# Order of a Strassen-style second MLP product against the LN2 of the next rows

## The chip, the cores and the metric

The kernel runs on one core of one Trainium2 chip. The metric is device time in microseconds (us) for one execution of the whole kernel; a kernel's time is the median of several executions. The engines run their own instruction streams and meet at semaphores: TensorE (PE in the profile) for matrix products, VectorE (DVE), ScalarE (ACT), GpSimd (POOL), and SyncE (SP), whose queue issues the DMA transfers. Each engine takes its compute instructions in the order in which the program gives them (this kernel is scheduled by hand: the order of the calls in the Python source is the order on every engine).

## The reference

One pre-norm block over 2048 rows of 576 values: a sliding dilated attention with 32 heads, then an MLP with 4608 hidden values, both with a residual. Cut to what matters here:

```python
def _layernorm(x): ...                       # mean and variance over the 576 columns
def _B_ref(x, w1, b1, w2, b2):
    y = _layernorm(x)
    h = _gelu(einsum("bsd,df->bsf", y, w1) + b1)
    return einsum("bsf,fd->bsd", h, w2) + b2

h  = x + _A_ref(_layernorm(x), wqkv, wo)     # _A_ref: attention, then the product with wo
h2 = h + _B_ref(_layernorm(h), w1, b1, w2, b2)
return h2
```

Operands are bf16; the MLP's inner `_layernorm` and the one in front of it are folded into one (called LN2 below).

## The kernel before

The 16 tiles of 128 rows are worked off in eight pairs (`GROUPS`). For each pair the MLP has two steps. `mlp1` makes the hidden values: PE products into PSUM (`pm`), GELU on ACT into `hT`. Then comes the product with w2. For the last two pairs, the seventh and the eighth, this second product is done as a Strassen-Winograd scheme with seven products instead of eight blocks' worth (`mlp2_fast`). Each of the seven has 18 matmuls of 128x128 by 128x288.

PSUM is used as four pairs of banks, tagged A, B, C and D:

```python
    def psum_pair(tag, name, dtype=F32):
        n = 512 if dtype == F32 else 1024
        return psum.tile([P, 2, n], dtype, tag=f"ps{tag}", name=name)
...
        PLAN = {
            "pair": [[([0], "A"), ([1], "B")], [([2], "D"), ([3], "C")], [([4], "A"), ([5], "B")],
                     [([6], "C"), ([7], "D"), ([8], "A")]],        # mlp1: visits and their banks
        }
```

The second product. `a` to `f` are accumulators, one bank each; product 1 is made once in `a` and is copied by ACT to `b`, so that it can be the start of two sums: product 2 is added to `a`, product 6 to `b`.

```python
    def h_sums(v):                  # four DVE sums and differences of hidden values, visit v
        ...
    PRODUCTS = {
        1: (lambda m: h_block(0, 0, m // 2)[:, m % 2, :], lambda m: w2_block(0, 0, m, m + 1)),
        2: (lambda m: h_block(1, 0, m // 2)[:, m % 2, :], lambda m: w2_block(1, 0, m, m + 1)),
        3: (lambda m: s_slot(3, m, m + 1), lambda m: w2_block(1, 1, m, m + 1)),
        4: (lambda m: h_block(1, 1, m // 2)[:, m % 2, :], lambda m: t_slot(3, m, m + 1)),
        5: (lambda m: s_slot(0, m, m + 1), lambda m: t_slot(0, m, m + 1)),
        6: (lambda m: s_slot(1, m, m + 1), lambda m: t_slot(1, m, m + 1)),
        7: (lambda m: s_slot(2, m, m + 1), lambda m: t_slot(2, m, m + 1)),
    }                               # s_slot: what h_sums wrote; t_slot: sums of w2, made earlier

    def product(n, bank, start, m0=0, m1=None): ...         # 18 matmuls into one bank

    def mlp2_fast(g, tags, last, ahead):
        j0, j1 = g
        call(ahead)
        h_sums(len(VISITS) - 1)
        af, b, ce, d = (psum_pair(tag, "po") for tag in tags)
        a, f, c, e = (pair[:, n, 0:HALF] for pair in (af, ce) for n in range(2))
        b, d = b[:, 0, 0:HALF], d[:, 0, 0:HALF]
        bank = {1: a, 2: a, 3: f, 4: c, 5: d, 6: b, 7: e}
        ...
        then = {
            1: [c_(nc.scalar.copy, b, a)],
            6: [c_(nc.scalar.copy, d, b)],
            2: [c_(add, o0[:, lo], a, x_all[:, j0, lo])] + ...,
            5: ..., 3: ...,
        }
        then.setdefault(6 if last else 7, []).extend([c_(residual), c_(add, o1[:, lo], c, rest[:, lo])])
        ...
        if last:
            order = [(1, 0, cut), (4, 0, cut), (1, cut, NM), (4, cut, NM)] + [(n, 0, NM) for n in (7, 6, 2, 5, 3)]
        else:
            order = [(n, 0, NM) for n in (1, 4, 2, 6, 7, 5, 3)]
        for n, m0, m1 in order:
            product(n, bank[n], n in (1, 3, 4, 7), m0, m1)
            if m1 == NM:
                call(then.get(n, ()))
```

For the seventh pair, `ahead` is the work on the rows of the eighth (c and d here are row tiles, not banks): the product with wo into the PSUM pairs B and C, then LN2 for both tiles.

```python
                ia[0] = ia.get(0, []) + [c_(wo_visit, (c, "B"), (d, "C")), c_(ln2_pair, c, d, e)]
...
        def ln2_pair(c, d, e, b2=True):
            for j in (c, d):
                ln2(j)              # DVE: h = pw + x, statistics; reads the PSUM of wo_visit
                ln2_rstd(j)         # POOL: power -1/2
                if j == d:
                    ln2_bias(c)     # DVE
                    send_h(c)       # ACT: hn = normalised h; DMA: to DRAM and back transposed (hnT)
                if b2:
                    add_b2(j)       # DVE
            ...
            ln2_bias(d)
            send_h(d)
```

`hnT` is what the `mlp1` of the eighth pair reads. That step follows the seventh pair's `mlp2_fast` on PE. For the eighth pair `ahead` is empty.

Of the kernel before, what the change touches and what calls it, by code (L numbers as in the profile page):

```python
# [17 lines left out]
def kernel(  # L18
# [12 lines left out]
    nc = tc.nc  # L31
# [13 lines left out]
    HALF = D // 2  # L45
# [45 lines left out]
# [3 lines that stand above are left out]
# [389 lines left out]
    NM = FT // 2  # L483
# [40 lines left out]
    def h_sums(v):  # L524
        m = (2 * VISITS[v][0], 2 * VISITS[v][-1] + 2)
        def op(t, a, b, alu):
            nc.vector.tensor_tensor(out=s_slot(t, *m), in0=a, in1=b, op=alu)  # L527
        a11, a12, a21, a22 = (h_tile[v][:, odd::2, i * P:(i + 1) * P] for i in range(2) for odd in range(2))
        op(0, a21, a22, ALU.add)
        op(1, s_slot(0, *m), a11, ALU.subtract)  # L530
        op(2, a11, a21, ALU.subtract)
        op(3, a12, s_slot(1, *m), ALU.subtract)
# [12 lines left out]
    def product(n, bank, start, m0=0, m1=None):  # L545
        lhs, rhs = PRODUCTS[n]
        for m in range(m0, NM if m1 is None else m1):
            l, r = lhs(m), rhs(m)
            l = l.rearrange("p m c -> p (m c)") if len(l.shape) == 3 else l
            r = r.rearrange("p m c -> p (m c)") if len(r.shape) == 3 else r  # L550
            nc.tensor.matmul(bank, lhsT=l, rhs=r, start=(start and m == 0), stop=(m == NM - 1), skip_group_check=True)  # L551

    def c_(fn, *a):
        return lambda: fn(*a)

    def mlp2_fast(g, tags, last, ahead):
        j0, j1 = g
        call(ahead)
        h_sums(len(VISITS) - 1)
        af, b, ce, d = (psum_pair(tag, "po") for tag in tags)  # L560
        a, f, c, e = (pair[:, n, 0:HALF] for pair in (af, ce) for n in range(2))
        b, d = b[:, 0, 0:HALF], d[:, 0, 0:HALF]
        bank = {1: a, 2: a, 3: f, 4: c, 5: d, 6: b, 7: e}
        o0, o1 = (late.tile([P, D], BF16, tag="o_sb", name="o_sb", bufs=2) for _ in range(2))
        rest, part = (sb.tile([P, D], F32, tag="h", name="rest", bufs=2) for _ in range(2))
        lo, hi = slice(0, HALF), slice(HALF, D)

        def add(out, x, y):
            nc.vector.tensor_tensor(out=out, in0=x, in1=y, op=ALU.add)

        def residual():
            add(rest[:].rearrange("p (g c) -> p g c", g=2), e.unsqueeze(1).to_broadcast([P, 2, HALF]),
                x_all[:, j1, :].rearrange("p (g c) -> p g c", g=2))
            add(rest[:, lo], b, rest[:, lo])

        def store(j, o, cols):
            nc.sync.dma_start(out=out3[:, j, cols], in_=o[:, cols])
# [4 lines that stand above are left out]
            2: [c_(add, o0[:, lo], a, x_all[:, j0, lo])] + ([c_(store, j0, o0, lo)] if last else []),  # L582
            5: [c_(add, o1[:, hi], d, rest[:, hi]), c_(store, j1, o1, slice(0, D)),
                c_(add, part[:, hi], d, x_all[:, j0, hi])],
            3: [c_(add, o0[:, hi], f, part[:, hi]), c_(store, j0, o0, hi if last else slice(0, D))],
        }
        then.setdefault(6 if last else 7, []).extend([c_(residual), c_(add, o1[:, lo], c, rest[:, lo])])
        cut = 12
        if last:
            order = [(1, 0, cut), (4, 0, cut), (1, cut, NM), (4, cut, NM)] + [(n, 0, NM) for n in (7, 6, 2, 5, 3)]  # L590
        else:
            order = [(n, 0, NM) for n in (1, 4, 2, 6, 7, 5, 3)]
        for n, m0, m1 in order:
            product(n, bank[n], n in (1, 3, 4, 7), m0, m1)
            if m1 == NM:
                call(then.get(n, ()))
# [9 lines left out]
    def call(fns):  # L606
        for fn in fns:
            fn()

    with tc.manual_schedule(engines={ENG.PE, ENG.Activation, ENG.DVE, ENG.SP, ENG.Pool}):  # L610
# [167 lines left out]
        def mlp1(grp, plan, ahead, between):  # L778
            for v, duos in enumerate(PLAN[plan]):
                call(ahead.get(v, ()))  # L780
                visit([mlp1_duo(grp, us, tag) for us, tag in duos], None, between.get(v, ()))

        def mlp2_tile(grp, i, tag, inserts):
            po_of[grp[i]] = psum_pair(tag, "po")
            mlp2(i, [po_of[grp[i]][:, half, 0:HALF] for half in range(2)], inserts)
# [17 lines left out]
        for k, g in enumerate(GROUPS):  # L803
            c, d = GROUPS[k + 1] if k + 1 < len(GROUPS) else (None, None)
            e, f = GROUPS[k + 2] if k + 2 < len(GROUPS) else (None, None)
            m1, mid, ia, ib = {}, {}, {}, {}
            m1[0] = []
            if 0 < k <= len(GROUPS) - len(fast):
                m1[0].append(c_(finish_out, GROUPS[k - 1][1]))
            if k == 0:  # L810
                m1[0] += [c_(halos, 1), c_(att_qk_a, d), c_(att_qk_b, d), c_(halo, d, 1)]
                mid[0] = [c_(exps, d)]
                m1[1] = [c_(pv_t, c), c_(pv_t, d), c_(load_w2, 4), c_(att_qk, e)]
                ia[0] = [c_(wo_visit, (c, "B"))]
                ia[12] = [c_(exps, e), c_(wo_visit, (d, "A")), c_(ln2_pair, c, d, e, False), c_(pv_sum, e), c_(dma_tr_o, e), c_(halos, 2)]
                ib[0] = [c_(finish_out, g[0])]
                ib[4] = [c_(att_qk, f)]
                ib[32] = [c_(exps, f)]
            elif c is not None:
                m1[0].append(c_(pv_t, d))  # L820
                if k == 1:
                    m1[0] += [c_(add_b2, j) for j in g]
                if e is not None:
                    m1[3] = m1.get(3, []) + [c_(att_qk, e)] + [c_(w2_sums, *m) for m in T_SUMS.get(k, ())]
                    ia[0] = [c_(exps, e)]
                ia[0] = ia.get(0, []) + [c_(wo_visit, (c, "B"), (d, "C")), c_(ln2_pair, c, d, e)]
                ib[0] = [c_(finish_out, g[0])]
                if e is not None:
                    ia[2] = [c_(pv_sum, e), c_(dma_tr_o, e)]
                    ib[2] = [c_(att_qk, f)] + ([c_(halos, 7)] if k == 1 else [])  # L830
                    ib[32] = [c_(exps, f)]
            if g in fast:
                if g == fast[0]:
                    m1[1] = [c_(w2_sums, 16, NM)]
                for v in range(3):
                    m1[v + 1] = m1.get(v + 1, []) + [c_(h_sums, v)]
            mlp1(g, "pair", m1, mid)
            if g in fast:
                mlp2_fast(g, "DBAC" if c is not None else "BDCA", c is None, ia.get(0, ()))
            else:  # L840
                mlp2_tile(g, 0, "D", ia)
                mlp2_tile(g, 1, "C", ib)
# [30 lines left out]
```

## Time and profile before

| | |
|---|---|
| time, median of 3 | 374.71 us (374.47 to 376.33) |
| span of the profiled execution | 374.5 us |
| PE busy | 364.6 us, 97% of the span |
| DVE busy | 315.9 us, 84% |
| ACT busy | 210.0 us, 56% |
| POOL busy | 26.5 us, 7% |
| mean granted clock of TensorE | 0.993 of full speed |

The page of the profile gives busy time, the chain of work that ended last, and groups of instructions. A group is named by its source line, engine and operation, then by what it writes and reads: "L551 PE MATMUL po<-w2a_sb,hT" are the matmuls of `product` that take their moving operand from `w2a_sb`; `po<-kv_ring,...`, `q_all` and `x_all` are those that take it from the sums of w2, which are kept in buffers no longer needed by the attention. "L554 ACT COPY po<-po" is the copy from one accumulator to another, "L168 ACT ACTIVATE hn" the normalisation of LN2, L402 the DVE addition that opens LN2, L527 the sums in `h_sums`, L204 all products of `mlp1` and wo, L569 the additions that make the output. A time in brackets is how long the engine stood idle before the row, with what released it.

### The profile page before, as it was taken

To read this page: it belongs to the slowest core of one execution; us is meant where nothing else is said; L and a number is where in the kernel's file an instruction comes from. 1 tells how busy PE (TensorE), PEld (TensorE's weight loads), DVE (VectorE), ACT (ScalarE), POOL (GpSimd) and SP (SyncE) were. 2 spreads that over 40 slices of the span, in tenths; PEclk is the share of its full clock that TensorE was granted. 3 is DMA by queue.
4 is the path that set the end of the run, shared out by engine and by line. 5 is a ranking of instruction groups with operands and counts; after the bars stand their busy time and mean duration, and the time that the engine had idled before them with its cause. 6 is when DMAs were issued, how large, how long until landed. Compare 5 with 4: busy or idle time off the path is not lost.

```text
span 374.5 us, 11470 instructions
## 1 busy us (share of the span) xinstructions
PE 364.6 (97%) x4944; PEld 301.0 (80%) x4944; DVE 315.9 (84%) x522; ACT 210.0 (56%) x435; POOL 26.5 (7%) x34
## 2 busy tenths in 40 slices
PE   7999999999999999999999999999999999799996
PEld 3789877887789978887888788878887788578874
DVE  6899999999999999999998999999999995632332
ACT  2688756796509851875187508760876087205630
POOL 2231004000100010002000200020002000200000
PEclk9999999999999999999999999999999999899999
DMA  8969798946335326412411241114110411110000
GB/s 246 311 193 292 186 189 256 338 143 102 125 88 161 38 54 185 156 35 54 102 52 35 55 102 52 35 38 118 52 35 19 109 45 21 39 47 20 4 0 32
DMA packets 57265, 38.96 MB, mean 104 GB/s; under 512 B 31344, under 2 KB 55536, under 8 KB 57216
## 3 DMA queue, kind: packets, MB, share of 16 engines
q1 hardware_dynamic: 57056, 38.18, 37.8%
q8 instruction: 38, 0.62, 0.7%
q14 instruction: 11, 0.09, 0.1%
q10 hardware_dynamic: 160, 0.07, 0.1%
HBM read 19.92 MB, written 12.42 MB: 86 GB/s over the span
## 4 chain that ended last, share of the span: by engine, by line
PE 67%; DVE 26%; issue 2%; POOL 2%; ACT 1%; DMA 1%; POOLq 0%; DVEq 0%
PE pm L204 31%; PE po L480 24%; PE po L551 8%; DVE prod L318 4%; DVE ln_stats L144 4%; PE pw L204 4%; DVE prod L357 3%; DVE prod L312 3%; DVE prod L361 3%; POOL ln_rstd L155 2%; DVE ln_mv L145 1%; PE pq L204 1%; DVE mx L328 1%; DVE h L402 1%; ACT hT L465 1%
## 5 line engine op out<-in xcount | busy, mean ns | idle before, releaser
L204 PE MATMUL pm<-hnT,w_sb 64*128 64x256 bf16 x2304 | 143.2, 269 | 0.6 <-ACT hT L465 0.5
L465 ACT ACTIVATE hT<-pm,b_sb 128x256 bf16<-128x256 f32 (+1 forms) x288 | 108.2, 503 | 34.2 <-PE pm L204 32.2
L204 PEld LDWEIGHTS <-w_sb 64*128 64x128 bf16 x2304 | 113.6, 94 | 14.4 <-issue 2.6
L480 PEld LDWEIGHTS <-hT 128*128 128x128 bf16 x864 | 84.0, 98 | 22.6 <-issue 1.7
L480 PE MATMUL po<-w2a_sb,hT 128*128 128x288 bf16 x672 | 84.5, 286 | 0.0
L204 PE MATMUL pq<-wq_sb,xnT 64*128 64x288 bf16 x768 | 54.1, 283 | 0.3 <-ACT kv_ring L289 0.2
L204 PEld LDWEIGHTS <-xnT 64*128 64x128 bf16 x864 | 44.0, 94 | 9.1 <-issue 0.4
L155 POOL TENSOR_TENSOR ln_rstd<-ln_veps,mhalf 128x1 f32<-128x1 f32 (+2 forms) x27 | 25.8, 957 | 296.1 <-DVE ln_veps L149 247.9
L318 DVE TENSOR_TENSOR prod<-prod 128x2304 bf16<-128x2304 bf16 (+1 forms) x64 | 44.2, 691 | 2.1
L340 ACT ACTIVATE logits<-logits 128x256 f32<-128x256 f32 x16 | 6.7, 417 | 67.9 <-DVE logits L329 67.9
L357 DVE TENSOR_TENSOR prod<-kv_ring,a 128x4608 bf16<-128x4608 bf16 x16 | 40.9, 2558 | 0.3
L312 DVE TENSOR_TENSOR prod<-kv_ring,q_all 128x4608 bf16<-128x4608 bf16 x16 | 40.8, 2552 | 0.2
L204 PE MATMUL pm<-hnT,w1h_sb 64*128 64x256 bf16 x288 | 39.5, 269 | 0.0
L361 DVE TENSOR_TENSOR prod<-prod 128x2304 bf16<-128x2304 bf16 (+1 forms) x32 | 33.9, 1058 | 1.1
L480 PE MATMUL po<-w2b_sb,hT 128*128 128x288 bf16 x192 | 25.5, 286 | 0.0
L289 ACT CAST kv_ring<-pq 128x576 bf16<-128x576 f32 x32 | 19.4, 641 | 8.3 <-PE pq L204 8.2
L168 ACT ACTIVATE hn<-h,ln_nmr,ln_rstd 128x576 bf16<-128x576 f32 x16 | 13.9, 867 | 15.6 <-DVE ln_nmr L164 15.6
L204 PE MATMUL pw<-wo_sb,oT 64*128 64x288 bf16 x256 | 19.5, 283 | 0.2
L438 ACT ACT_TABLE_LOAD x14 | 18.0, 1283 | 0.3
L204 PEld LDWEIGHTS <-oT 64*128 64x128 bf16 x288 | 14.1, 94 | 4.0 <-POOLq L214 0.8
L527 DVE TENSOR_TENSOR prod<-hT 128x512 f16<-128x512 f16 (+1 forms) x8 | 3.6, 455 | 16.1 <-ACT hT L465 16.1
L402 DVE TENSOR_TENSOR h<-pw,x_all 128x576 f32<-128x576 f32 x16 | 12.0, 752 | 5.7 <-PE pw L204 5.7
(88 smaller groups left out, 317.1 us busy)
## 6 DMA issues: line engine op xcount, KB each, us to landing
w_sb<-in_B_w_dram SPq DMA_DIRECT2D x6, 768.0 KB, 6.1
kv_ring<-kv_dram SPq DMA_DIRECT2D x28, 144.0 KB, 2.5
w2a_sb<-in_B_w_dram SPq DMA_DIRECT2D x4, 1008.0 KB, 6.3
kv_dram<-kv_ring SPq DMA_DIRECT2D x13, 288.0 KB, 4.1
out_dram<-o_sb SPq DMA_DIRECT2D x15, 144.0 KB, 2.0
td<-q_all SPq DMA_DIRECT2D x14, 144.0 KB, 2.3
td<-hn SPq DMA_DIRECT2D x14, 144.0 KB, 2.0
wq_sb<-in_A_wqkv_dram SPq DMA_DIRECT2D x3, 576.0 KB, 5.8
```

Source lines behind the costliest of these rows:

```text
L155: nc.gpsimd.tensor_tensor(out=rstd[:], in0=veps[:], in1=mhalf[:].to_broadcast([P, n]), op=ALU.pow)
L204: last = nc.tensor.matmul(duo["g"][r ^ swap][i], lhsT=lhsT, rhs=rhs, start=(swap == 0 and i == 0 and kt == 0), stop=(swap == 1 and kt == K ...
L289: pace[0] = nc.scalar.copy(out=dst.rearrange("p (d g h) -> p g d h", g=2, h=H // 2), in_=ps[:, :, 0:HALF].rearrange("p g (h d) -> p g d h" ...
L312: nc.vector.tensor_tensor(out=prod[:], in0=k_ring[j % 2], in1=q_all[:, j, :].unsqueeze(1) .to_broadcast([P, W, D]), op=ALU.mult)
L318: nc.vector.tensor_tensor(out=prod[:, :, o * H:o * H + n], in0=prod[:, :, a * H:a * H + n], in1=prod[:, :, c * H:c * H + n], op=ALU.add)
L357: nc.vector.tensor_tensor(out=prod[:].rearrange("p w (d h) -> p w d h", h=H), in0=v_ring[j % 2].rearrange("p w (d h) -> p w d h", h=H), in ...
L361: nc.vector.tensor_tensor(out=prod[:, 0:n, :], in0=prod[:, 0:n, :], in1=prod[:, n:2 * n, :], op=ALU.add)
L402: nc.vector.tensor_tensor(out=h[:].rearrange("p (g c) -> p g c", g=2), in0=pw[:, :, 0:HALF], in1=x_all[:, j, :].rearrange("p (g c) -> p g ...
L438: nc.scalar.activation(out=warm[:], in_=mhalf[:], func=ACT.Gelu_apprx_tanh)
L465: pace[0] = nc.scalar.activation(out=hT[us[i // GF]][:, GF * r + i % GF, 0:N], in_=ps[:, r, i * N:(i + 1) * N], func=ACT.Gelu_apprx_tanh, ...
L480: nc.tensor.matmul(banks[half], lhsT=hT[f // (2 * GF)][:, f % (2 * GF), i * P:(i + 1) * P], rhs=w2_rows(f)[:, half * HALF:(half + 1) * HAL ...
L551: nc.tensor.matmul(bank, lhsT=l, rhs=r, start=(start and m == 0), stop=(m == NM - 1), skip_group_check=True)
```

## The change

In the second product of the seventh pair, product 1 and its copy are now issued between the two parts of `ahead`: after the product with wo, ahead of LN2. The rest of the seven products follow after LN2 and `h_sums` as before, without product 1. Because `b` is now taken while B and C still hold the result of the wo product that LN2 has to read, the bank tags are dealt out anew: `b` moves from B to A, and the pair of `c` and `e` from A to B; `a`, `f` and `d` stay where they were. The purpose is that the copy stands ahead of LN2's two normalisations in the order of ACT. The eighth pair's order doesn't change, since its `ahead` is empty and it is excepted by `if not last`.

```diff
     def mlp2_fast(g, tags, last, ahead):
         j0, j1 = g
-        call(ahead)
+        call(ahead[:1])
+        af, b = (psum_pair(tag, "po") for tag in tags[:2])
+        if not last:
+            product(1, af[:, 0, 0:HALF], True)
+            nc.scalar.copy(out=b[:, 0, 0:HALF], in_=af[:, 0, 0:HALF])
+        call(ahead[1:])
         h_sums(len(VISITS) - 1)
-        af, b, ce, d = (psum_pair(tag, "po") for tag in tags)
+        ce, d = (psum_pair(tag, "po") for tag in tags[2:])
         a, f, c, e = (pair[:, n, 0:HALF] for pair in (af, ce) for n in range(2))
...
         else:
-            order = [(n, 0, NM) for n in (1, 4, 2, 6, 7, 5, 3)]
+            order = [(n, 0, NM) for n in (4, 2, 6, 7, 5, 3)]
...
             if g in fast:
-                mlp2_fast(g, "DBAC" if c is not None else "BDCA", c is None, ia.get(0, ()))
+                mlp2_fast(g, "DABC" if c is not None else "BDCA", c is None, ia.get(0, ()))
```

## The prediction

> **What bounds the kernel now.** I read the page first: PE is busy 364.6 of 374.5 us, so only its idle or slow stretches can give time back. The busy shares in 40 slices show one dent late in the run.
>
> ```profile
> PE   7999999999999999999999999999999999799996
> ...
> PEclk9999999999999999999999999999999999899999
> ```
>
> Slice 35 (about 318 to 328 us) has a 7 for PE and an 8 for the clock granted to it: one place, with both an idle stretch and a slow one. It lies in the second product of the seventh pair. The list of who waited for whom, for PE from 295 us to the end, names one wait.
>
> ```profile
> PE po L551 <- ACT po L554: 2.3, 1, 2.3
> ```
>
> So a matmul waited once, for 2.3 us, for the ACT copy of product 1. The timeline of that stretch shows which matmul and why the copy was late.
>
> ```profile
> 317.81 1.89 PE L551 MATMUL po<-w2a_sb,hT 128*128 128x288 bf16 x14
> 319.53 0.65 PE L551 MATMUL po<-w2b_sb,hT 128*128 128x288 bf16 x4
> ...
> 320.02 1.14 PE L551 MATMUL po<-kv_ring,hT 128*128 128x288 f16 x8
> ...
> 321.98 0.41 PE L551 MATMUL po<-kv_ring,hT 128*128 128x288 f16 x2
> ...
> 322.19 0.87 ACT L168 ACTIVATE hn<-h,ln_nmr,ln_rstd 128x576 bf16<-128x576 f32 x1 [3.74 <-DVE ln_nmr L164]
> ...
> 323.46 0.87 ACT L168 ACTIVATE hn<-h,ln_nmr,ln_rstd 128x576 bf16<-128x576 f32 x1 [0.40 <-DVE ln_nmr L164]
> ...
> 324.24 0.39 ACT L554 COPY po<-po 128x288 f32<-128x288 f32 x1
> ...
> 324.68 3.10 PE L551 MATMUL po<-w2a_sb,hT 128*128 128x288 bf16 x14 [2.29 <-ACT po L554]
> 327.57 1.14 PE L551 MATMUL po<-w2b_sb,hT 128*128 128x288 bf16 x4
> ```
>
> Product 1 (w2 blocks: 14 + 4 matmuls) runs from 317.81 and ends at 319.53 + 0.65 = 320.18. Product 4 (w2 sums) fills PE until 322.39. Product 2 comes next and adds to the bank that the copy has to read first. The copy's input is ready at 320.18, but ACT stands 3.74 us idle in front of the first normalisation of LN2, which is ahead of the copy in its order and waits for DVE. The copy starts at 324.24, 4.06 us later than its data allow.
>
> The view by stretches tells what happens to the clock after the gap (columns: stretch, length, busy time and count of PE, PEld, DVE, ACT, POOL, then clock, DMA share, GB/s).
>
> ```profile
> 322.40:324.68 2.28, 0.01 (x1) 0.00 (x1) 1.80 (x5) 1.82 (x3) 0.83 (x1) 1.00 0.24 72
> 324.68:328.50 3.82, 3.82 (x18) 2.50 (x18) 0.74 (x2) 0.00 (x0) 0.00 (x0) 0.56 0.34 86
> 328.50:337.46 8.96, 8.96 (x73) 6.96 (x71) 2.95 (x6) 0.38 (x1) 0.00 (x0) 1.00 0.16 38
> ```
>
> The 18 matmuls of product 2 run at a mean clock of 0.56; cut into half microseconds, the same view has 0.50 in every piece from 325.5 to 328.5, and 0.94 in the next. So the wait costs twice: as a gap, and as a slow product after it.
>
> [...]
>
> **The change, part by part.**
>
> *Removed: the gap.* Matmuls of this shape start every 2.20 / 18 = 0.122 us (in the eighth pair product 2 starts at 364.09 and the next product at 366.29). Product 4's last piece starts at 321.98 and has 2 matmuls, so the next could start at 321.98 + 0.24 = 322.22. It started at 324.68: **2.46 us** lost. (The profile's 2.29 counts from the modelled end.)
>
> *Removed: the slow product.* Product 2 takes from 324.68 to the start of product 6 at 328.53, 3.85 us, against 2.20 us at full clock: **1.65 us** lost. If PE no longer idles, its clock has no reason to fall.
>
> Cross-check: from product 1 to the first matmul of the next mlp1 is 337.46 - 317.81 = 19.65 us. Seven undisturbed products are 7 x 2.20 = 15.40 us, and about 0.24 us of issue time stands ahead of mlp1 in the trace. 19.65 - 15.40 - 0.24 = 4.01 us, against 2.46 + 1.65 = 4.11. I take 4.1.
>
> *Moved: product 1.* On PE it already followed the wo product directly, with only DVE, ACT, POOL and DMA work standing between them in program order. Its place on PE, 317.81, doesn't move: 0 us.
>
> *Moved: the copy.* It should start about 0.09 us after product 1 ends, as in the eighth pair (359.10 to 359.19), so at 320.27, and take 0.39 us, ending near 320.66. Product 2 wants its bank at 322.22, so there are some 1.5 us to spare. ACT is idle from 318.45 (the last GELU, 313.96 + 4.49) to 322.19, so the copy delays no normalisation: 0 us.
>
> *Moved: the banks.* `b` now takes A, last read by GELU on ACT until 318.45, before the copy. `c` takes B, last read by the L402 addition at 317.43 + 0.76 = 318.19; product 4 wants it at 320.02. In the eighth pair's mlp1, A and B are the first pairs wanted, and the last readers of `b`, `c` and `e` are the additions after product 7, all done (335.04 in the old trace) before product 3 is through. The swap costs nothing.
>
> *Added:* no instruction; the counts are the same. Sum: 374.71 - 4.1 = 370.6 us, a ratio of 0.989.
>
> **The rivals.**
>
> 1. *Another wait takes the gap's place: h_sums.* Product 6 moves up to 322.22 + 2.20 = 324.42. Its last third needs the second L527 result of the last visit, which ends at 323.93 + 0.56 = 324.49, and is wanted at 324.42 + 12 x 0.122 = 325.9. Product 7 needs the third (324.95) only after 326.6. Even a wait put on the first matmul would cost 0.1 us. Slack against: 1.4 us. If DVE were 2 us later, the time would be near 371.3 to 372.
>
> 2. *Transposed rows for the next mlp1 arrive late.* The last transpose is issued at 328.70, and the transfer view gives 3.0 us to landing: 331.7. The next mlp1 moves from 337.46 to 333.4. Slack 1.7 us, so a transfer up to that much slower is still hidden. If it came 2 us late, the time would be 371. LN2 itself isn't touched, so I see no reason for that.
>
> 3. *The clock doesn't come along.* If its dip had another cause than the gap, only 2.46 us would be won: 372.3. Against: every long stretch around it stands at 1.00, with the same matmuls and the same load, and the dip begins half a microsecond after the gap.
>
> 4. *The gain is given back at the tail.* The eighth pair's products follow its mlp1 on PE without a wait, and the last output addition ends with product 3. The chain after 324.68 is PE alone (12.86, 17.79 and 15.56 us, then one DVE addition of 0.46). Nothing there is tied to an absolute time, so the shift should arrive whole.
>
> 5. *Slower*: the copy would have to hold up LN2, and LN2 the mlp1, by over 4 us beyond their slack. I see nothing for it.
>
> **Range and chances.** The central value is 370.6. Rivals 1 and 2 in mild form would add up to 1 us, rival 3 makes 372.3; the three times before spread from 374.47 to 376.33, so a median can sit half a microsecond off or more. On the low side there is only the reading error of the sum, a few tenths. I take 370.1 to 371.9. Faster by over 2% would need 7.5 us, where all that can be won here is 4.1; slower by over 2% needs a new wait that I don't find. Chances: 0.01 faster, 0.98 within 2%, 0.01 slower.
>
> **What would show each step right or wrong.** The wait "PE po L551 <- ACT po L554" disappears from the list of PE's waits. The first copy stands at about 320.3, ahead of both hn rows, and these stay at about 322.2 and 323.5. Product 2 starts near 322.2 and takes 2.2 us; the clock is 1.00 from 322 to 334. The next mlp1 starts at about 333.4, the last product's end moves up by 4.1, and the span is about 370.4 us. The prediction is wrong if PE shows a new wait, on L527 or before the first matmul of mlp1, or if the clock still falls to half somewhere in 322 to 330.

## The result and the profile after

The changed kernel takes 372.23 us in the median of four executions (372.02 to 372.65), the kernel before 374.75 us (374.47 to 376.33). The ratio is 0.9926, with a 95% interval of 0.9896 to 0.9955. The prediction was 370.6 us with a range of 370.1 to 371.9: the change is an improvement, as foretold, but of 2.5 us instead of 4.1, and the time lies outside the range.

And yet the trace after looks as the prediction drew it. The page's rows for PE and its clock have lost both dents:

```profile
PE   7999999999999999999999999999999999999996
...
PEclk9999999999999999999999999999999999999999
```

In the list of who waited for whom, PE has no row for L551 any more. The timeline of the stretch (start, length, what) has the copy, now line L562, ahead of both normalisations:

```profile
318.32 1.89 PE L551 MATMUL po<-w2a_sb,hT 128*128 128x288 bf16 x14
...
320.04 0.65 PE L551 MATMUL po<-w2b_sb,hT 128*128 128x288 bf16 x4
...
320.79 0.38 ACT L562 COPY po<-po 128x288 f32<-128x288 f32 x1 [1.83 <-PE po L551]
...
322.49 0.41 PE L551 MATMUL po<-kv_ring,hT 128*128 128x288 f16 x2
...
322.70 0.87 ACT L168 ACTIVATE hn<-h,ln_nmr,ln_rstd 128x576 bf16<-128x576 f32 x1 [1.53 <-DVE ln_nmr L164]
322.74 1.88 PE L551 MATMUL po<-w2a_sb,hT 128*128 128x288 bf16 x14
...
323.97 0.87 ACT L168 ACTIVATE hn<-h,ln_nmr,ln_rstd 128x576 bf16<-128x576 f32 x1 [0.40 <-DVE ln_nmr L164]
...
324.94 1.14 PE L551 MATMUL po<-kv_ring,prod 128*128 128x288 f16 x8
```

This execution is 0.51 us later than the old one when product 1 starts (318.32 against 317.81), for reasons upstream. From there, the copy starts 0.10 us after product 1 ends (320.04 + 0.65 = 320.69), product 2 follows product 4 in the very next slot, and takes 324.94 - 322.74 = 2.20 us. The stretches show the full clock where it was 0.56:

```profile
322.40:324.68 2.28, 2.28 (x21) 1.83 (x19) 1.77 (x7) 1.57 (x2) 0.99 (x1) 1.00 0.10 32
324.68:328.50 3.82, 3.82 (x34) 3.04 (x32) 1.63 (x4) 0.54 (x2) 0.00 (x0) 1.00 0.30 73
```

The chain of work that ended last goes from the wo product through all seven products into the next mlp1 on PE alone (columns: start, length, what):

```profile
316.18 2.21 PE pw L204 x36
318.38 15.54 PE po L551 x126
333.93 17.79 PE pm L204 x324
351.72 15.56 PE po L551 x126
367.30 0.46 DVE o_sb L574
```

Before, it left PE for LN2 and came back through the copy, behind which stood 90 of the 126 matmuls of `product`:

```profile
323.46 0.02 ACT hn L168
...
324.24 0.40 ACT po L554
...
324.68 12.86 PE po L551 x90
```

From product 1 to the next mlp1 there are now 333.93 - 318.32 = 15.61 us, where there were 19.65: 4.04 us less between these two traces, as predicted. The puzzle is therefore not in the kernel after. The two traces differ by 4.0 us in this stretch and by 3.6 us in their spans (374.5 and 370.9), but the two medians only by 2.5 us.

The lead is a pair of numbers for single executions. The profiled execution of the kernel before has a span of 374.5 us and a time of 376.27 us; the other one has 370.9 and 372.65. A time is some 1.8 us longer than the span of the same execution. So the profiled execution of the kernel before was not a 374.7 us one but one of 376.3, although its span looks like the median.

### The profile page after: what moved, and what is told of

Its sections match the earlier page's. It is cut to its first block, busy times and chain, and to the rows that moved or that the text cites. A ratio compares the mean times of both kernels' runs of the same rounds, so it can differ in the third digit from the quotient of the medians.

```text
span 370.9 us, 11469 instructions
## 1 busy us (share of the span) xinstructions
PE 363.7 (98%) x4944; PEld 300.7 (81%) x4944; DVE 316.0 (85%) x522; ACT 209.7 (57%) x435; POOL 26.5 (7%) x34
## 4 chain that ended last, share of the span: by engine, by line
PE 71%; DVE 22%; issue 2%; ACT 1%; DMA 1%; POOL 1%; POOLq 0%; DVEq 0%
PE pm L204 31%; PE po L480 24%; PE po L551 8%; PE pw L204 4%; DVE prod L357 3%; DVE prod L318 3%; DVE prod L312 3%; DVE prod L361 3%; DVE ln_stats L144 2%; PE pq L204 2%; DMA kv_ring<-kv_dram 1%; PE busy L636 1%; POOL ln_rstd L155 1%; DVE mx L328 1%; ACT hT L465 1%
## 5 line engine op out<-in xcount | busy, mean ns | idle before, releaser
L527 DVE TENSOR_TENSOR prod<-hT 128x512 f16<-128x512 f16 (+1 forms) x8 | 3.6, 455 | 16.0 <-ACT hT L465 16.0
```

## The theory and its rivals

**Theory T**: the gap on PE is there in every execution of the kernel before, and costs 2.46 us. The half clock after it, 1.65 us, is met only in some; the profiled one was among them, and the median of four was not. **R1**: all 4.1 us are won in every execution, and the new banks or the moved product lose 1.6 us again. **R2**: every gap, however short, brings the clock down. **R3**: the clock's fall has nothing to do with the length of the gap. **R4**: it comes from the wait or the load after it, not from PE's idleness.

In all, 101 more executions of the kernel before were timed beside the experiments. They fall into two groups with nothing between: 56 with a mean granted clock of 0.998 to 1.000 and a median of 374.70 us (374.41 to 375.70), and 45 with 0.993 to 0.995 and a median of 376.41 us (376.09 to 378.01). The medians lie 1.71 us apart; product 2 at half clock had been worked out as 1.65. The profiled execution of the kernel before has (1 - 0.56) / 0.5 x 3.82 = 3.4 us at half clock; that takes about 3.4 x 0.5 / 374.5 = 0.005 off the mean clock, which is the distance between the groups. Below, "with the clock down" means an execution of the second kind; where in the run its clock was down is seen in the profiled executions alone. The time exceeds the span by 1.79 us in the mean of the 101 (1.73 to 1.86).

## The experiments

### The copy put back

```diff
             product(1, af[:, 0, 0:HALF], True)
-            nc.scalar.copy(out=b[:, 0, 0:HALF], in_=af[:, 0, 0:HALF])
         call(ahead[1:])
+        if not last:
+            nc.scalar.copy(out=b[:, 0, 0:HALF], in_=af[:, 0, 0:HALF])
```

> The changed kernel with the copy put back behind LN2 on ACT; product 1 stays ahead of LN2 in the program and the new bank tags stay. Theory (T): the copy's place on ACT is all that the change is worth, and the second term of the prediction, 1.65 us of half-clock matmuls after the gap, is paid only in some executions, so that the median never held it. T expects the gap of 2.3 to 2.5 us back, a median of about 374.7 us (ratio to the kernel before 1.000), single executions either near 374.6 or near 376.3, and a mean granted clock near 0.998 in the first kind and near 0.993 in the second. Rival (R1): the whole 4.1 us was won in every execution, and the new banks or the moved product cost some 1.6 us elsewhere; then this kernel stands at about 376.3 us, ratio 1.004.

Measured: 375.82 us in the median of 22 executions, beside 375.70 for the kernel before; ratio 1.0007 (0.9990 to 1.0023). Half of them, 11 of 22, had the clock down (376.12 to 377.06 us), and the other 11 had 374.43 to 375.53. The timeline of one with the clock down shows the old picture:

```profile
322.33 0.41 PE L551 MATMUL po<-kv_ring,hT 128*128 128x288 f16 x2
...
324.58 0.39 ACT L564 COPY po<-po 128x288 f32<-128x288 f32 x1
325.03 3.49 PE L551 MATMUL po<-w2a_sb,hT 128*128 128x288 bf16 x14 [2.28 <-ACT po L564]
```

The gap is back, 325.03 - (322.33 + 0.24) = 2.46 us, and with it both groups. With the clock up, the medians are 374.66 us here and 374.70 for the kernel before. So the new banks and the place of product 1 in the program bring nothing that shows by themselves; the gain comes with the copy's place on ACT. R1 needed a ratio of 1.004, which the interval excludes. T's median of 374.7 was a miss of its own kind: with the two groups of equal size, a median falls anywhere between them.

### The copy between the two normalisations

```diff
-            nc.scalar.copy(out=b[:, 0, 0:HALF], in_=af[:, 0, 0:HALF])
+            mid_ln2.append(lambda: nc.scalar.copy(out=b[:, 0, 0:HALF], in_=af[:, 0, 0:HALF]))
...
                     send_h(c)
+                    while mid_ln2:
+                        mid_ln2.pop()()
```

> The changed kernel with the copy between the two normalisations of LN2 on ACT: after the first hn, ahead of the second. The copy should start about 0.8 us after the first hn starts and the gap on PE be about 1.2 us. T expects 372.2 + 1.2 = 373.4 us (ratio 0.996 to 0.997), a linear price of the gap, and no execution with the clock at half after so short a gap. A rival (R2) in which every gap trips the clock expects 372.2 + 1.2 + 1.65 = 375.1 us.

Measured: 373.45 us (373.15 to 373.82), ratio 0.9941 (0.9918 to 0.9964), and no execution of 6 with the clock down. Product 2 starts at 323.25 where it could have at 322.07, a gap of 1.18 us:

```profile
321.83 0.41 PE L551 MATMUL po<-kv_ring,hT 128*128 128x288 f16 x2
...
323.25 1.88 PE L551 MATMUL po<-w2a_sb,hT 128*128 128x288 bf16 x14 [1.01 <-ACT po L564]
```

372.26 us, the median of the changed kernel in the later comparison, plus 1.18 is 373.44. (The ratio came out below the expected 0.996 because the kernel before had a median of 375.70 in this comparison.) R2 falls: this gap costs its own length and no more.

### The gap made longer

```diff
         call(ahead)
+        for _ in range(0 if last else 2):          # 6 in the other kernel
+            nc.scalar.copy(out=idle[:], in_=b2_bc[:, 0:256])
         h_sums(len(VISITS) - 1)
```

`idle` is a scratch tile that nobody reads; both are edits of the kernel before.

> The kernel before, with two ACT copies of 128x256 elements put in front of the copy of product 1 (some 0.3 us each), so that the gap on PE is about 3.0 to 3.2 us in place of 2.46. Nothing else is touched. T expects the median at 374.75 + 0.6 = 375.4 us when the clock stays up and at 377.0 when it falls, and a larger part of the executions with the clock down than in the kernel before (half or more). If the clock's fall has nothing to do with the gap's length (R3), it is met as seldom as before and the median is 375.4.

> As the run before, with six such copies, about 1.8 us more: a gap of about 4.3 us. T expects every execution to have the half clock after the gap: 374.75 + 1.8 + 1.65 = 378.2 us, ratio 1.009, mean granted clock about 0.99. R3, a linear price alone: 376.6 us, ratio 1.005, with the clock at 1.00 in most executions.

Measured with two copies: 376.87 us (375.20 to 378.52), ratio 1.0019 (1.0004 to 1.0034), gap 3.19 us. 15 of 22 executions had the clock down, beside 21 of 43 of the kernel before, which alone would not decide. The median of the other seven is 375.43, which is 374.70 plus the 0.73 us by which the gap is longer.

Measured with six: 379.39 us (378.73 to 380.16), ratio 1.0096 (1.0071 to 1.0121). The copies took 0.43 us each, not 0.3, so the gap is 4.93 us; all 6 executions had the clock down, at 0.989 to 0.995. With this gap T's sum is 374.70 + 2.47 + 1.71 = 378.9 us; the two executions at 0.995 took 378.73 and 378.74 us, the four at 0.989 or 0.990 took 379.32 us and more. R3 falls: it expected the full clock in most of these executions. In the profiled one, at 0.995, the clock stays up through the whole gap and falls only after PE has started again, for (1 - 0.56) / 0.5 x 3.85 = 3.4 us:

```profile
321.98 0.41 PE L552 MATMUL po<-kv_ring,hT 128*128 128x288 f16 x2
...
327.15 3.32 PE L552 MATMUL po<-w2a_sb,hT 128*128 128x288 bf16 x14 [4.76 <-ACT po L555]
```

```profile
322.30:327.15 4.85, 0.09 (x2) 0.00 (x1) 2.64 (x6) 4.23 (x9) 0.93 (x1) 1.00 0.22 58
327.15:331.00 3.85, 3.85 (x18) 2.54 (x18) 0.00 (x0) 0.00 (x0) 0.00 (x0) 0.56 0.41 99
```

The profiled execution with two copies had a mean clock of 0.990, and shows why that is less than 0.994. Its clock stays down for about 6.8 us (0.9 + 4.25 + 1.7 in the stretches below), not 3.4, so that product 6 is slow as well:

```profile
322.22 0.41 PE L552 MATMUL po<-kv_ring,hT 128*128 128x288 f16 x2
...
325.65 3.52 PE L552 MATMUL po<-w2a_sb,hT 128*128 128x288 bf16 x14 [3.02 <-ACT po L555]
...
328.96 1.17 PE L552 MATMUL po<-w2b_sb,hT 128*128 128x288 bf16 x4
329.92 1.94 PE L552 MATMUL po<-kv_ring,prod 128*128 128x288 f16 x8
331.70 0.65 PE L552 MATMUL po<-q_all,prod 128*128 128x288 f16 x4
```

```profile
322.50:325.65 3.15, 0.13 (x3) 0.00 (x0) 2.67 (x6) 2.66 (x5) 0.97 (x1) 0.85 0.17 52
325.65:329.90 4.25, 4.25 (x18) 2.69 (x18) 0.01 (x1) 0.00 (x0) 0.00 (x0) 0.50 0.33 79
329.90:331.70 1.80, 1.80 (x9) 1.16 (x8) 0.46 (x1) 0.00 (x0) 0.00 (x0) 0.54 0.45 99
331.70:337.00 5.30, 5.30 (x46) 4.24 (x44) 1.46 (x3) 0.38 (x1) 0.00 (x0) 1.00 0.00 0
```

Here the clock had fallen before the gap was over: the mean of 0.85 makes 0.9 us at half clock, and a piece of half a microsecond, cut out of the gap, has 0.50 with PE idle:

```profile
325.00:325.50 0.50, 0.00 (x0) 0.00 (x0) 0.50 (x2) 0.50 (x2) 0.00 (x0) 0.50 0.00 0
```

So in this execution the load after the gap can't have brought it down. Nor does the clock fall a fixed time after PE stops: here it fell some 2.3 us after that, with six copies later than 4.9 us.

### The changed kernel again

> The changed kernel as it is, timed beside many executions of the kernel before, which in the last comparison split into 22 of 374.4 to 375.7 us with a clock of 0.998 or more and 21 of 376.2 to 377.0 us with 0.993 to 0.995. T expects one group only, 372.0 to 373.3 us, clock never below 0.998: 2.46 us under the first group of the kernel before and 4.1 us under the second. R1 (the gain is partly given back in the changed kernel) expects executions of the changed kernel near 370.6 as well.

Measured: 372.26 us (372.04 to 372.67), 6 executions, clock 0.998 to 1.000 in each; ratio 0.9914 (0.9889 to 0.9939) beside 36 executions of the kernel before, 13 of them with the clock down. With the first four there are ten of the changed kernel, all in one group. It lies 374.70 - 372.26 = 2.44 us under the first group of the kernel before, and 376.41 - 372.26 = 4.15 us under the second: the gap alone, and the gap with the slow product. No execution came near 370.6.

### The gap filled with matmuls nobody needs

```diff
         for n, m0, m1 in order:
+            if n == 2 and not last:
+                lhs, rhs = PRODUCTS[1]
+                for m in range(14):
+                    nc.tensor.matmul(f, lhsT=lhs(m), rhs=rhs(m).rearrange("p m c -> p (m c)"), start=True, stop=True,
+                                     skip_group_check=True)
             product(n, bank[n], n in (1, 3, 4, 7), m0, m1)
```

> The kernel before, order, copy and banks untouched, with 14 matmuls more between products 4 and 2 that write into the bank of f, where product 3 starts afresh later: their result is thrown away. The wait for the copy stays and ends when it did, but PE is idle for 2.46 - 14 x 0.122 = 0.75 us only. T expects 374.5 to 375.7 us in every execution and a clock of 0.998 or more: the wait alone, without the second price. If the half clock came from the wait itself or from the load after it and not from PE's idleness (R4), about half of the executions would stand at 376.2 to 377.0 as before, or later by what the extra matmuls cost.

Measured: 377.35 us (376.24 to 378.29), ratio 1.0054 (1.0038 to 1.0070), 4 of 15 executions with the clock down, beside 13 of 36 of the kernel before. It was a miss, because the gap was not filled. PE's list of waits has the new line, L597, behind the copy:

```profile
PE po L597 <- ACT po L554: 2.3, 1, 2.3
```

The bank of `f` belongs to the same pair, and the same tile of the program, as that of `a`, and its writers waited for the reader of `a`. So 14 x 0.122 = 1.71 us were only added: 374.70 + 1.71 = 376.4. The median of the 11 with the clock up is 377.23, of their spans 374.8 instead of 372.9; in some of them the time exceeds the span by up to 2.95 us in place of 1.8, and the cause of that is open. As a filled gap it tells T and R4 apart in nothing. But its profiled execution, with a mean clock of 1.00, shows what no other trace here does: the gap at its old length, 324.60 - (321.91 + 0.24) = 2.45 us, with full speed after it, 14 matmuls in 1.71 us.

```profile
321.91 0.41 PE L551 MATMUL po<-kv_ring,hT 128*128 128x288 f16 x2
...
324.60 1.88 PE L597 MATMUL po<-w2a_sb,hT 128*128 128x288 bf16 x14 [2.28 <-ACT po L554]
...
326.31 1.88 PE L551 MATMUL po<-w2a_sb,hT 128*128 128x288 bf16 x14
```

The same matmuls into the bank of `e`, in a pair that the copy doesn't touch, in the kernel before and in the one with six ACT copies (there 30 of them):

> In the earlier filling of the gap the 14 matmuls wrote into the second bank of the pair that holds a, and the trace shows them behind the wait for the copy, so that PE's gap was not filled. Here they write into the bank of e, in a pair that the copy doesn't touch, where product 7 starts afresh later. They should run from about 322.2 to 323.9 and leave 0.75 us of idleness; the wait for the copy ends when it did. T expects 374.5 to 375.7 us and a clock of 0.998 or more in every execution, against 43% of the kernel before with the clock down (34 of 79). R4 (the dip comes from the wait or the load after it, not from idleness) expects the same share of dips as before.

> The kernel with six ACT copies ahead of the copy of product 1 (gap 4.93 us, clock down in all 6 executions, 378.7 to 380.2 us), with 30 discarded matmuls into the bank of e in the gap: 30 x 0.122 = 3.66 us of it filled, 1.27 us left idle. The wait for the copy is as long as it was. T expects no dip at all and 374.6 + (4.93 - 2.46) = 377.1 us (376.9 to 378.2). R4 expects the clock down in every execution, and 378.7 us or more.

Measured for the kernel before: 375.22 us (374.58 to 376.19), ratio 0.9990 (0.9975 to 1.0005). The matmuls run in the gap, and what is left at its end is 325.29 - (322.84 + 1.71) = 0.74 us:

```profile
322.84 1.88 PE L597 MATMUL po<-w2a_sb,hT 128*128 128x288 bf16 x14
...
324.85 0.39 ACT L554 COPY po<-po 128x288 f32<-128x288 f32 x1
...
325.29 1.88 PE L551 MATMUL po<-w2a_sb,hT 128*128 128x288 bf16 x14 [0.57 <-ACT po L554]
327.00 0.65 PE L551 MATMUL po<-w2b_sb,hT 128*128 128x288 bf16 x4
```

None of 14 executions had the clock down, beside 11 of 22 of the kernel before; two stand at 0.997, just under the 0.998 expected. The median span is 372.9 us, as in the first group of the kernel before. The times, though, exceed the spans by up to 3.2 us, as with the matmuls in the bank of `f`; three lie above the 375.7 expected, and no gain in time is shown (the interval holds 1).

Measured for the long gap: 377.22 us (377.06 to 378.42), ratio 1.0044 (1.0026 to 1.0063), 9 executions, none with the clock down. Without the 30 matmuls the same wait had given 379.39 and the clock down in all 6. After 4.93 us of waiting, of which 1.27 idle, product 2 runs at full speed:

```profile
322.59 3.84 PE L600 MATMUL po<-w2a_sb,hT 128*128 128x288 bf16 x30
...
327.53 1.88 PE L552 MATMUL po<-w2a_sb,hT 128*128 128x288 bf16 x14 [1.10 <-ACT po L555]
```

```profile
327.53:331.00 3.47, 3.47 (x29) 2.77 (x29) 0.46 (x1) 0.00 (x0) 0.00 (x0) 1.00 0.27 69
```

R4 falls. The wait and the load after it were the same, and only PE's idleness was less. Work thrown away makes that kernel 2.2 us shorter (ratios to the kernel before, timed beside each: 1.0096 and 1.0044).

### A gap of 1.9 us

```diff
                     send_h(c)
+                    for _ in range(2 if mid_ln2 else 0):
+                        nc.scalar.copy(out=idle[:], in_=b2_bc[:, 0:256])
                     while mid_ln2:
```

> As the copy between the two normalisations (gap 1.18 us, no execution of 6 with the clock down), with two ACT copies of 128x256 ahead of it: a gap of about 1.9 us. The shares of executions with the clock down were 0 at 1.18, 0.49 at 2.46, 0.68 at 3.2 and all 6 at 4.9 us of gap. Two readings: a straight line from 1.18 to 2.46 expects a share near 0.28. A reading [...] fits 0.49 and 0.68 and expects none at 1.9 us. Time of an execution without a dip: 372.2 + 1.9 = 374.1 us; with one: 375.8 us.

Measured: 374.23 us (373.93 to 376.41), ratio 0.9969 (0.9954 to 0.9984); the gap is 1.92 us, and 372.26 + 1.92 = 374.18.

```profile
322.40 0.41 PE L552 MATMUL po<-kv_ring,hT 128*128 128x288 f16 x2
324.56 1.88 PE L552 MATMUL po<-w2a_sb,hT 128*128 128x288 bf16 x14 [1.75 <-ACT po L565]
```

One execution of 22 had the clock down, beside 13 of 36 of the kernel before. A straight line would have given six; the other reading, an estimate of the author's fitted to the shares at 2.46 and 3.2 us, none. All gaps together:

| idle gap on PE | executions with the clock down | median time without it |
|---|---|---|
| none (changed kernel) | 0 of 10 | 372.26 us |
| 1.18 us | 0 of 6 | 373.45 |
| 1.92 us | 1 of 22 | 374.18 |
| 2.46 us (kernel before) | 45 of 101 | 374.70 |
| 2.46 us (copy put back) | 11 of 22 | 374.66 |
| 2.45 us (14 matmuls behind it) | 4 of 15 | 377.23, with more work |
| 3.19 us | 15 of 22 | 375.43 |
| 4.93 us | 6 of 6 | none |

The last column rises by the length of the gap, from row to row, but for the row with more work. The middle column is a lottery whose odds jump between 1.9 and 2.5 us: 1 of 22 at 1.92, 45 of 101 at 2.46. The profiled dips last 3.4 us (the kernel before, the copy put back, six copies) or 6.8 us (two copies); with two copies the clock falls 0.9 us before the gap is over, with six about 0.2 us after it. What decides whether an execution has a dip is not shown.

## Why the prediction was wrong, step by step

**What bounds the kernel: right.** The one wait on PE after 295 us, its cause (the copy behind LN2's normalisations in ACT's order, started 4.06 us after its data were there) and its cure are confirmed by the copy put back.

**"Removed: the gap", 2.46 us: right.** 2.44 us between the groups with the clock up.

**"Removed: the slow product", 1.65 us: the size is right, its place in the sum is not.** It is 1.71 us where it occurs. But it occurs in 45 of 101 executions, and it was subtracted as though it were in all.

**The step that failed is the sum: "374.71 - 4.1 = 370.6 us".** It takes a cost read in one execution off a median made of others. The profiled execution was a 376.27 us one: 376.27 - 4.1 = 372.2, which is what was measured. The error was hidden by the difference of 1.8 us between time and span, which made a span of 374.5 look like the median of 374.71. It could have been found beforehand: the three times before, 374.47, 374.71 and 376.33, stood in two places, 1.6 to 1.9 us apart, the profiled execution had taken 376.27 us, and 1.65 us was the very term that had been worked out. The prediction took this spread for scatter.

**Moved product, moved copy, moved banks, "0 us" each: right.** Ratio 1.0007 with product and banks moved and the copy not; the normalisations stood at 322.70 and 323.97, which is 322.19 and 323.46 plus the 0.51 us of this execution.

**Rival 1 (h_sums) and rival 4 (tail): rightly put aside.** No wait on L527 appeared, and the eighth pair's chain is as long as before. **Rival 2 (transposed rows)**: the last transpose was issued at 329.72, 0.5 us later than foreseen after allowing for the shift, and landed 2.8 us later, at 332.5; the slack was 1.4 us instead of 1.7, and held.

**Rival 3 gave the right number, 372.3 us, for a wrong reason.** It asked whether the dip had a cause other than the gap. None shows: with the gap gone or filled, the clock was down in none of 10 + 14 + 9 executions. What the rival lacked was the third possibility, that the gap is its cause in only some executions. The argument against it, that the dip begins right after the gap, was true, and no answer to how often.

Also wrong in the text: "So the wait costs twice". In the kernel before it cost twice in 45 of 101 executions.

## What to carry to other kernels

Before a cost seen in one trace is taken off a median, put the traced execution's own time and mean granted clock beside the other executions: if it is a slow one of two kinds, the costs that make it so are not in the median. In this kernel a gap on PE has a fixed price, its length, and a price by chance, some 1.7 us of half clock or, with the clock down for 6.8 us, about 3 (378.42 us against 375.43), which was met in none of 6 executions at 1.18 us of idleness, 1 of 22 at 1.92 and 45 of 101 at 2.46; to bring this gap from 2.46 us to 1.92 or less is worth more than its microseconds. ACT took its operations in the order of the program, and the copy, whose data were there at 320.18 us, started at 324.24, after two normalisations that had waited for DVE: a short operation that another engine waits for goes ahead of those that wait themselves.

## What was not expected

Of the hardware: that discarded matmuls can pay. 30 of them in a gap of 4.93 us took the time from 379.39 to 377.22 us; 14 in the gap of 2.46 us kept the clock up, but brought no clear gain in time. And that the clock dip has two lengths in the profiled executions, 3.4 us in three and 6.8 us in one. In the one long dip that was profiled, 0.9 us of the gap lay behind the fall of the clock; in the three short ones 0.1 us at most. Whether that makes the difference is not shown.
